# Splitting the large weight pieces with TensorE, and filling the routing lists ten steps earlier

## The chip, the cores and the metric

One core of one Trainium2 chip runs one program. The metric is the device time of one execution in microseconds (us); the time of a kernel is the median of its runs. The kernel before takes 1601.51 us (three runs, 1599.92 to 1602.22).

## The reference

Three layers follow each other on 4608 tokens (8 batches of 576) of width 512. The first is attention over pooled keys: every 8 keys and 8 values are averaged, so each of the 8 heads has 72 of them.

```
k_p = k.reshape(B, H, Sp, 8, D).mean(axis=3);  v_p likewise
attn = softmax(q @ k_p.T / sqrt(D));  x = attn @ v_p          # as rows of 512
```

The second is a feed-forward layer of width 2048 whose activation is a quotient of two polynomials.

```
h = x @ w_in                                   # 512 -> 2048
g = (a0 + a1 h + a2 h^2 + a3 h^3) / (1 + |b0||h| + |b1|h^2 + 1e-6)
x = g @ w_out                                  # 2048 -> 512
```

The third sends each token to one of 8 experts (the largest of 8 logits), runs relu(x @ w1[e]) @ w2[e] with inner width 1024, and scales by the gate.

`w_in` and `w_out` come in 64-bit floats (read as pairs of 32-bit words), all other inputs in 32-bit floats.

## The kernel before, in words

Accuracy is kept by splitting each matrix operand into a high part (float32r, a reduced form that TensorE takes in one pass) and a low part (what the high part leaves over); a product is then three matmuls, high by high, high by low, low by high.

The program has a front, a main loop and a tail. **The front** (before the first `mm1`) does the attention of the first units and turns 24 of the 40 weight pieces into split weights. **The main loop** has steps t = 0, 1, 2, ...; each does one 128-wide slice of the feed-forward layer for a block of 384 tokens (`mm1`, the polynomials in `act_a` to `act_d`, then `mm2` of the slice three steps back, LAG = 3), 16 slices to a block, 12 blocks; attention of later blocks goes on beside it. At the end of a block `evac` copies three results out of PSUM (`y0`, `y1`, `y2`) into buffers of the tag `ys` and writes them to the rows `yd` in DRAM; routing then scatters token numbers into the list `ids`. **The tail** runs the experts.

All engines take their instructions in the order in which the code issues them; nothing is reordered. `point(p)` issues the attention events due at point p (8 points to a unit of 384 tokens and two heads, two points to a step), `tick(c)` issues what is due of the weight pieces at tick c. In the front a tick comes every PACE = 1.3 points from point P0 on, HEAD = 27 ticks in all; from then on there is one tick per step.

A large piece c (c < 24, `j < RING`) is 128 x 512 doubles in a ring of 8 SBUF slots (`sr`). Its chain is spread over the ticks by the table `CONV`:

- tick c: `conv_magnitude` (ScalarE) writes the upper words, scaled, to a PSUM buffer `mag` (tags `y0` to `y3` in turn);
- tick c+1: `conv_sign` (GpSimd) leaves a signed zero in the upper word;
- tick c+2: `conv_join` (VectorE, two instructions) puts sign, exponent and mantissa together as a 32-bit float, into the ring slot for even c and into `mag` for odd c;
- tick c+3: `conv_high` (ScalarE) writes the high part into `wt`; `conv_low` subtracts it from the float and writes the low part, on GpSimd for even c, on VectorE for odd c.

Small pieces (c from 24 on, 128 x 256, buffers `s64` of the tag `ys`) go one tick faster, with the low part on GpSimd. Loads are issued ahead on the DMA queue of SyncE (SP): four ticks ahead for large pieces, one for small ones.

`clear_lists` and `clear_rows` fill `ids` with a mark and the rows of the last two batches in `yd` with zeros: a memset each on GpSimd, then DMAs. They run at step t = NFC + 2 = 18, from two of the three buffers of the tag `ys`, at whose end the first `evac` runs. `kvl` is the pool of three buffers (tag `kv`) into which keys and values are loaded; in the points of steps 8 to 19 no such load is due. `Q`, a PSUM buffer of the tag `y3`, is used by `act_c` in every step of the main loop, and by nothing in the front but `mag`.

Of the kernel before, what the change touches and what calls it, by code (L numbers as in the profile page):

```python
# [9 lines left out]
F32 = mybir.dt.float32  # L10
F32R = mybir.dt.float32r
BF16 = mybir.dt.bfloat16
I32 = mybir.dt.int32
# [3 lines left out]
AF = mybir.ActivationFunctionType  # L17
ALU = mybir.AluOpType
# [91 lines left out]
def tile_kernel(  # L110
# [15 lines left out]
    nc = tc.nc  # L126
    B, H, S, _ = q.shape
    NT, DM = out.shape
    DFF = w_in.shape[1]
    NFC = DFF // 128  # L130
# [14 lines left out]
    one = ctx.enter_context(tc.tile_pool(name="one", bufs=1))  # L145
# [3 lines left out]
    ysp = ctx.enter_context(tc.tile_pool(name="ysp", bufs=3))  # L149
    sm = ctx.enter_context(tc.tile_pool(name="sm", bufs=2))  # L150
    dr = ctx.enter_context(tc.tile_pool(name="dr", bufs=1, space=DRAM))
    py = ctx.enter_context(tc.tile_pool(name="py", bufs=1, space=PSUM))
# [5 lines left out]
    kvl = first.enter_context(tc.tile_pool(name="kvl", bufs=3))  # L158
# [3 lines left out]
    def f32(x):  # L162
        return x.bitcast(F32)
# [8 lines left out]
    def con(name):  # L172
        o, w = cols[name]
        return cst[:, o:o + w]

    ident = con("ident")
    ones = one.tile([G, G], BF16, name="ones")
    nc.vector.memset(ones, 1.0)
    tri = one.tile([G, G], BF16, name="tri")
    make_upper_triangular(nc, tri, val=1.0, diag=False)  # L180
    ab = one.tile([128, 6], F32, name="ab")
# [18 lines left out]

    def clear_lists():
        w = DM
        none = ysp.tile([128, w], I32, tag="ys", name="none")
        nc.gpsimd.memset(none, 2 * NT)
        fill = (E * NT + SL) // 128
        idf = ids.rearrange("(p n) o -> p (n o)", n=fill)
        for o in range(0, 2 * fill, w):
            nc.sync.dma_start(idf[:, o:min(o + w, 2 * fill)], none[:, :min(w, 2 * fill - o)])

    def clear_rows():  # L210
        zero = ysp.tile([96, DM], F32, tag="ys", name="zero")
        nc.gpsimd.memset(zero, 0.0)
        nc.sync.dma_start(yd[(B - 2) * S:, :].rearrange("(p r) c -> p r c", p=96),
                          zero.unsqueeze(1).to_broadcast([96, 2 * S // 96, DM]))
# [13 lines left out]
    wt, cv = {}, {}  # L228
    RING = 6

    def pieces():
        for j in range(NPW):
            w = 512 if j < RING else 256
            for i in range(2):
                for o in range(0, 1024, w):
                    yield j, i, o, w

    PIECES = list(pieces())
# [19 lines left out]
    def words(c):  # L258

        w = cv[c][0].bitcast(U32).rearrange("p (n t) -> p n t", t=2)  # L260
        return w[:, :, 0], w[:, :, 1]

    def conv_magnitude(c):


        j, i, o, w = PIECES[c]
        if i == 0 and o == 0:
            wt[j] = wp.tile([128, 4, 1024], F32R, tag="w", name="wt")
        if j < RING:
            m = py.tile([128, 512], F32, tag=f"y{c % 4}", name="mag")  # L270
        else:
            if "room" not in cv:
                cv["room"] = ysp.tile([128, KD, G], F32, tag="yT", name="mag", bufs=1)
            m = cv["room"][:, c % 2 * 2:c % 2 * 2 + 2].rearrange("p a b -> p (a b)")
        nc.scalar.activation(m, words(c)[1].bitcast(F32), AF.Copy, scale=2.0 ** -112)
        cv[c][1] = m.bitcast(U32)
# [6 lines left out]
    def conv_join(c):  # L283

        (low, up), mag = words(c), cv[c][1]
        nc.vector.scalar_tensor_tensor(out=mag, in0=mag, scalar=3, in1=up,
                                       op0=ALU.logical_shift_left, op1=ALU.bitwise_or)
        out_ = mag if PIECES[c][0] < RING and c % 2 else low
        nc.vector.scalar_tensor_tensor(out=out_, in0=low, scalar=29, in1=mag,
                                       op0=ALU.logical_shift_right, op1=ALU.bitwise_or)  # L290
        cv[c][2] = out_.bitcast(F32)

    def conv_high(c):
        j, i, o, w = PIECES[c]
        nc.scalar.activation(wt[j][:, 2 * i, o:o + w], cv[c][2], AF.Copy)

    def conv_low(c):
        j, i, o, w = PIECES[c]
        (nc.vector if j < RING and c % 2 else nc.gpsimd).tensor_tensor(
            out=wt[j][:, 2 * i + 1, o:o + w], in0=cv.pop(c)[2], in1=f32(wt[j][:, 2 * i, o:o + w]), op=ALU.subtract)  # L300

    CONV = ((0, 0, conv_magnitude), (3, 2, conv_high), (1, 0, conv_sign), (2, 1, conv_join), (3, 2, conv_low))
    TICKS = NCV + 2
    BIG, AHEAD = RING * 4, 4
    loaded = [0]
# [6 lines left out]
    def tick(c):  # L314
        for big, small_, fn in CONV:
            for x in sorted({c - big, c - small_}):
                if 0 <= x < NCV and x == c - (big if x < BIG else small_):
                    fn(x)
        load_to(min(c + AHEAD, max(BIG + 2, c + 1)))
# [215 lines left out]
    def point(p):  # L535
        for fn, U in agenda.get(p, ()):
            fn() if U is None else fn(U)
        if extra and extra[0][0] <= p and (p % 8 in (6, 7) or p > last_unit):
            extra.pop(0)[1](p)
# [4 lines left out]
    def mm1(n, fc):  # L544
        hps = ph.tile([128, N], F32, tag="h", name="hps")
        t, fl = wt[fc // 2], fc % 2
        i, last = 0, 3 * KD - 1
        for wi, xi in ((0, 0), (0, 1), (1, 0)):
            for kk in range(KD):
                nc.tensor.matmul(hps, lhsT=w_in_part(t, wi, kk, fl), rhs=xT[n, kk][:, xi, :],  # L550
                                 start=(i == 0), stop=(i == last))
                i += 1
        return hps

    def act_a(t, hps):
        A = elp.tile([128, N], F32, tag="A", name="A")
        nc.scalar.activation(A, hps, AF.Abs)  # L557
        el[t] = A, hps
# [17 lines left out]
    def act_c(t, part):  # L576

        if part == 0:
            A, C = el[t]
            Q = py.tile([128, N], F32, tag="y3", name="Q")  # L580
            nc.scalar.activation(Q, A, AF.Ln, bias=qone)
            nc.scalar.activation(Q, Q, AF.Exp, scale=-1.0)  # L582
            nc.vector.scalar_tensor_tensor(out=C, in0=C, scalar=a0, in1=Q, op0=ALU.add, op1=ALU.mult)  # L583
            nc.vector.scalar_tensor_tensor(out=Q, in0=A, scalar=qone, in1=Q, op0=ALU.add, op1=ALU.mult)
            el[t] = Q, C
        else:
            Q, C = el[t]
            nc.vector.scalar_tensor_tensor(out=C, in0=Q, scalar=-2.0, in1=C, op0=ALU.add, op1=ALU.mult)  # L588

    def act_d(t):  # L590
        _, C = el.pop(t)
        hi = t3p.tile([128, N], F32R, tag="hi", name="hi")
        lo = t3p.tile([128, N], F32R, tag="lo", name="lo")
        nc.scalar.activation(hi, C, AF.Copy)  # L594
        nc.gpsimd.tensor_tensor(out=lo, in0=C, in1=f32(hi), op=ALU.subtract)  # L595
        gT[t] = hi, lo
# [432 lines left out]


    total = NFC * NBLK
    P0, PACE, HEAD = 4, 1.3, BIG + 3
    c = 0
    for p in range(min(agenda), LEAD):
        if p == min(agenda) + 1:
# [8 lines left out]
    for t in range(total + main.end):  # L1044
        g = t - total - 1
        if g == -NFC:
            first.close()
            p2["one"] = ctx.enter_context(tc.tile_pool(name="p2", bufs=1))
            p2["stg"] = ctx.enter_context(tc.tile_pool(name="stg", bufs=4))
            p2["xr"] = ctx.enter_context(tc.tile_pool(name="xrp", bufs=2))  # L1050
        if t == NFC + 2:
            clear_lists()
            clear_rows()
        point(2 * t + LEAD)
        if t < total:
            hps = mm1(*divmod(t, NFC))
        if g > 0:
            main.high(g)
            main.low(g)
        main.front(g)  # L1060
        if 2 <= t < total + 2:
            act_d(t - 2)
        if 1 <= t < total + 1:
            act_c(t - 1, 0)
        if t < total:
            act_a(t, hps)
        point(2 * t + 1 + LEAD)
        if t < total:
            act_b(t, 0)
        if 1 <= t < total + 1:  # L1070
            act_c(t - 1, 1)
        if t < total:
            act_b(t, 1)
        if g <= 0:
            main.high(g)
        if c < TICKS:
            tick(c)
            c += 1
        if g <= 0:
            main.low(g)  # L1080
        main.prepare(g)
        if LAG <= t < total + LAG:
            mm2(t - LAG)
            n, fc = divmod(t - LAG, NFC)
            if fc == NFC - 1:
                evac(n)
                extra += after_block(n, 2 * t + LEAD + (4 if n < NBLK - 1 else 2))
        main.back(g)
    left = nc.values_load(p2["over"][0:1, 0:1], min_val=0, max_val=NR)  # L1089
# [36 lines left out]
```

## Time and profile before

| | |
|---|---|
| median of 3 runs | 1601.51 us |
| profiled execution | 1602.74 us, of which the span of the trace is 1601.0 us |
| PE busy | 1501.1 us (94% of the span) |
| VectorE (DVE) busy | 1181.1 us (74%) |
| ScalarE (ACT) busy | 1066.4 us (67%) |
| GpSimd (POOL) busy | 756.0 us (47%) |
| mean granted TensorE clock | 0.973 of full speed |

The table is a mean over stages. The 40 slices of the page show the exceptions to a PE that is busy 90% or more: the first four slices (160 us), one slice near 200 us, and the end. PE = TensorE matmuls, PEld = its weight loads, SPq = the DMA queue of SyncE. A granted clock of 1.00 is 2.4 GHz, 0.50 is 1.2 GHz. Line numbers (L299) are those of the kernel before; in rows of the changed kernel's order the same lines stand up to 13 further down.

### The profile page before, as it was taken

The page shows a single profiled execution, that of the slowest core. Times are in us where ns is not written, and L with a number is a line of the kernel's source. Part 1 is how long each engine was busy: PE and PEld are TensorE (multiplying, and loading weights), DVE is VectorE, ACT ScalarE, POOL GpSimd, SP SyncE. Part 2 cuts the span into 40 slices and gives each one's busy share as a digit, 9 for nine tenths or more (in the row PEclk, how much of TensorE's full clock was granted, in tenths as well). Part 3 has the DMA queues.
Part 4 walks back from the last instruction along what each step waited for, and adds up shares of the span by engine and source line. Part 5 has one row for each costly group of instructions (what it writes and reads, how often), then busy time and mean ns, then how long its engine had stood idle before and what let it go on. Part 6 is the DMA issues. An engine that isn't in the chain of part 4 may idle for free. (4 is left out here: it accounts for less than half of the span.)

```text
span 1601.0 us, 25780 instructions
## 1 busy us (share of the span) xinstructions
PE 1501.1 (94%) x8636; PEld 1340.5 (84%) x8636; DVE 1181.1 (74%) x2325; ACT 1066.4 (67%) x2116; POOL 756.0 (47%) x865
## 2 busy tenths in 40 slices
PE   5678979999999999999999999999999999999995
PEld 4567868888889888898888898989899998999994
DVE  5869858878788878878888878778766666666661
ACT  4558856777777777777676777778465556565651
POOL 7958635656455655546565644456121212212210
PEclk9779989999999999999999999999999999999998
DMA  9421131211021111101121101023587777777760
GB/s 291 149 79 57 32 109 31 60 40 46 11 45 36 54 32 40 31 11 56 40 56 33 41 11 31 1 86 93 162 245 258 237 229 246 240 243 237 234 214 19
DMA packets 145995, 166.68 MB, mean 104 GB/s; under 512 B 54719, under 2 KB 97855, under 8 KB 145857
## 3 DMA queue, kind: packets, MB, share of 16 engines
q1 hardware_dynamic: 138624, 145.54, 29.8%
q0 software_dynamic: 7232, 19.44, 3.3%
q8 instruction: 70, 1.15, 0.3%
q14 instruction: 69, 0.56, 0.1%
HBM read 143.37 MB, written 22.09 MB: 103 GB/s over the span
## 5 line engine op out<-in xcount | busy, mean ns | idle before, releaser
L550 PE MATMUL hps<-xT,wt 128*128 128x384 f32 x2304 | 454.4, 346 | 0.0
L550 PEld LDWEIGHTS hps<-xT,wt 128*128 128x128 f32 x2304 | 407.9, 192 | 7.5 <-issue 0.3
L606 PE MATMUL y<-wt,hi 128*128 128x512 f32 x1152 | 372.4, 404 | 11.6 <-ACT ys L619 8.8
L573 POOL TENSOR_TENSOR A<-A,Bt 128x384 f32<-128x384 f32 x192 | 195.1, 1016 | 325.1 <-ACT Bt L572 306.6
L907 DVE TENSOR_TENSOR wt<-ws,wt 128x1024 fp32r<-128x1024 f32 x168 | 203.8, 1225 | 70.5 <-ACT wt L902 65.9
L606 PEld LDWEIGHTS y<-wt,hi 128*128 128x128 f32 x1152 | 204.8, 189 | 51.5 <-ACT ys L619 10.4
L595 POOL TENSOR_TENSOR lo<-C,hi 128x384 fp32r<-128x384 f32 x192 | 198.6, 1034 | 74.7 <-ACT hi L594 45.1
L606 PE MATMUL y<-wt,lo 128*128 128x512 f32 x576 | 227.5, 395 | 0.0
L916 PEld LDWEIGHTS h2ps<-x2T,wt 128*128 128x128 f32 x1632 | 213.0, 190 | 11.6 <-DVE lo L929 0.6
L949 PE MATMUL o<-wt,hi 128*128 128x512 f32 x608 | 220.0, 403 | 0.5 <-ACT hi L928 0.5
L916 PE MATMUL h2ps<-x2T,wt 128*128 128x256 f32 x1632 | 217.5, 283 | 0.5 <-DVE x2T L880 0.3
L583 DVE SCALAR_TENSOR_TENSOR C<-C,ab,Q 128x384 f32<-128x384 f32 x192 | 117.7, 613 | 134.3 <-ACT Q L582 131.3
L594 ACT ACTIVATE hi<-C 128x384 fp32r<-128x384 f32 x192 | 100.2, 522 | 146.6 <-DVE C L588 127.5
L902 ACT ACTIVATE wt<-ws 128x1024 fp32r<-128x1024 f32 x168 | 175.0, 1057 | 0.9 <-DMA ws<-in_moe_w_dram 0.9
L928 ACT ACTIVATE hi<-h2ps 128x256 fp32r<-128x256 f32 x136 | 52.3, 385 | 170.0 <-PE o L949 166.3
L572 ACT ACTIVATE Bt<-A,ab 128x384 f32<-128x384 f32 x192 | 136.5, 711 | 2.7 <-DVE ti L776 2.7
L949 PEld LDWEIGHTS o<-wt,hi 128*128 128x128 f32 x608 | 114.5, 188 | 20.9 <-ACT hi L928 0.7
L565 ACT ACTIVATE C<-hps,ab 128x384 f32<-128x384 f32 x192 | 129.8, 676 | 1.2
L866 POOL DMA_INDIRECT xr<-yd,at x38 | 46.8, 1232 | 174.9 <-PE xps L877 91.7
L606 PEld LDWEIGHTS y<-wt,lo 128*128 128x128 f32 x576 | 108.5, 188 | 24.5
L566 DVE TENSOR_TENSOR C<-C,hps 128x384 f32<-128x384 f32 x192 | 105.0, 547 | 30.0 <-ACT C L565 27.8
L557 ACT ACTIVATE A<-hps 128x384 f32<-128x384 f32 x192 | 93.8, 488 | 43.1 <-PE hps L550 42.1
(381 smaller groups left out, 2500.5 us busy)
## 6 DMA issues: line engine op xcount, KB each, us to landing
ws<-in_moe_w_dram SPq DMA_DIRECT2D x168, 512.0 KB
kt<-in_k_dram SPq DMA_DIRECT2D x64, 144.0 KB
yd<-ys SPq DMA_DIRECT2D x32, 256.0 KB
sr<-in_moe_w_in_dram SPq DMA_DIRECT2D x12, 512.0 KB
sr<-in_moe_w_out_dram SPq DMA_DIRECT2D x12, 512.0 KB
qt<-in_q_dram SPq DMA_DIRECT2D x64, 96.0 KB
vt<-in_v_dram SPq DMA_DIRECT2D x32, 144.0 KB
vt<-in_v_dram SPq DMA_DIRECT2D x32, 112.0 KB
```

The lines of the kernel that those rows point to most:

```text
L550: nc.tensor.matmul(hps, lhsT=w_in_part(t, wi, kk, fl), rhs=xT[n, kk][:, xi, :], start=(i == 0), stop=(i == last))
L565: nc.scalar.activation(C, hps, AF.Identity, scale=a3, bias=a2)
L566: nc.vector.tensor_tensor(out=C, in0=C, in1=hps, op=ALU.mult)
L572: nc.scalar.activation(Bt, A, AF.Identity, scale=b1, bias=b0)
L573: nc.gpsimd.tensor_tensor(out=A, in0=A, in1=Bt, op=ALU.mult)
L583: nc.vector.scalar_tensor_tensor(out=C, in0=C, scalar=a0, in1=Q, op0=ALU.add, op1=ALU.mult)
L595: nc.gpsimd.tensor_tensor(out=lo, in0=C, in1=f32(hi), op=ALU.subtract)
L606: nc.tensor.matmul(yps[n][r], lhsT=g[gi][:, r * G:(r + 1) * G], rhs=w_out_part(w, wi, fl), start=(fc == 0 and i == 0), stop=(fc == NFC - 1 ...
L902: nc.scalar.activation(s["wt"][j][:, 2 * i, :], s["ld"][c], AF.Copy)
L907: nc.vector.tensor_tensor(out=t[:, 2 * i + 1, :], in0=w, in1=f32(t[:, 2 * i, :]), op=ALU.subtract)
L916: nc.tensor.matmul(hps, lhsT=a_, rhs=b_, start=(i == 0), stop=(i == 3 * KD - 1))
L949: nc.tensor.matmul(s["o"][j], lhsT=hl[gi][:, x * 128:(x + 1) * 128], rhs=w_out_part(wt_, wi, fl), start=(first_ and n_ == 0), stop=(last_ ...
```

## The change

The low part of a large piece is no longer subtracted on GpSimd or VectorE. TensorE adds it up in PSUM, the float times the unit matrix `ident`, then the high part times `minus` (the unit matrix times -1), and ScalarE copies it out one tick later (`conv_left`). The sum stands in a single PSUM buffer, tag `y3`; `mag` keeps `y0` to `y2`. The joined float always goes into the ring slot. The front has 28 ticks in place of 27, at 1.25 points each. The two fills run at step 8 in place of 18, from buffers of the tag `kv`.

```diff
+    minus = one.tile([128, 128], F32R, name="minus")
+    nc.scalar.activation(minus, ident, AF.Copy, scale=-1.0)
...
     def clear_lists():
-        none = ysp.tile([128, w], I32, tag="ys", name="none")
+        none = kvl.tile([128, w], I32, tag="kv", name="none")
...
     def clear_rows():
-        zero = ysp.tile([96, DM], F32, tag="ys", name="zero")
+        zero = kvl.tile([96, DM], F32, tag="kv", name="zero")
...
-            m = py.tile([128, 512], F32, tag=f"y{c % 4}", name="mag")
+            m = py.tile([128, 512], F32, tag=f"y{c % 3}", name="mag")
...
-        out_ = mag if PIECES[c][0] < RING and c % 2 else low
-        nc.vector.scalar_tensor_tensor(out=out_, in0=low, scalar=29, in1=mag,
+        nc.vector.scalar_tensor_tensor(out=low, in0=low, scalar=29, in1=mag,
...
     def conv_low(c):
         j, i, o, w = PIECES[c]
-        (nc.vector if j < RING and c % 2 else nc.gpsimd).tensor_tensor(
-            out=wt[j][:, 2 * i + 1, o:o + w], in0=cv.pop(c)[2], in1=f32(wt[j][:, 2 * i, o:o + w]), op=ALU.subtract)
+        x, hi = cv.pop(c)[2], wt[j][:, 2 * i, o:o + w]
+        if j >= RING:
+            nc.gpsimd.tensor_tensor(out=wt[j][:, 2 * i + 1, o:o + w], in0=x, in1=f32(hi), op=ALU.subtract)
+            return
+        left = py.tile([128, 512], F32, tag="y3", name="left")
+        nc.tensor.matmul(left, lhsT=ident, rhs=x, start=True, stop=False)
+        nc.tensor.matmul(left, lhsT=minus, rhs=hi, start=False, stop=True)
+        cv["left", c] = left
+
+    def conv_left(c):
+        j, i, o, w = PIECES[c]
+        if j < RING:
+            nc.scalar.activation(wt[j][:, 2 * i + 1, o:o + w], cv.pop(("left", c)), AF.Copy)
-    CONV = ((0, 0, conv_magnitude), (3, 2, conv_high), (1, 0, conv_sign), (2, 1, conv_join), (3, 2, conv_low))
+    CONV = ((4, 3, conv_left), (0, 0, conv_magnitude), (3, 2, conv_high), (1, 0, conv_sign), (2, 1, conv_join), (3, 2, conv_low))
...
-    P0, PACE, HEAD = 4, 1.3, BIG + 3
+    P0, PACE, HEAD = 4, 1.25, BIG + 4
...
-        if t == NFC + 2:
+        if t == NFC // 2:
             clear_lists()
             clear_rows()
```

TensorE in the front, around the second unit, before. `vps` and `kps` pool values and keys, `qps` and `pps` are transposes, `sps` are scores, `ops` the output of attention.

```order
L411 MATMUL vps<-vt,cst 128x64 x8
L438 MATMUL qps<-cst,qt 128x128 x3
L479 MATMUL pps<-cst,pt 128x128 x3
L479 MATMUL pps<-cst,pt 16x128 x3
L405 MATMUL kps<-cst,kt 64x72 x8
L449 MATMUL sps<-kbd,qT 128x144 x3
```

The same stretch of TensorE's order in the changed kernel:

```order
L424 MATMUL vps<-vt,cst 128x64 x8
L306 MATMUL left<-sr,cst 128x512
L307 MATMUL left<-wt,minus 128x512
L451 MATMUL qps<-cst,qt 128x128 x3
L306 MATMUL left<-sr,cst 128x512
L307 MATMUL left<-wt,minus 128x512
L492 MATMUL pps<-cst,pt 128x128 x3
L306 MATMUL left<-sr,cst 128x512
L307 MATMUL left<-wt,minus 128x512
L492 MATMUL pps<-cst,pt 16x128 x3
L418 MATMUL kps<-cst,kt 64x72 x8
```

Between any two groups of attention matmuls there now stands a pair that needs the piece's float (VectorE), its high part (ScalarE) and the single buffer `left`.

ScalarE in the same stretch of the changed kernel (before, only the `mag` and `wt<-sr` or `wt<-mag` rows stood between those of attention):

```order
L313 ACTIVATE wt<-left 128x512
L277 ACTIVATE mag<-sr 128x512
L296 ACTIVATE wt<-sr 128x512
L453 ACTIVATE qT<-qps 128x384
L313 ACTIVATE wt<-left 128x512
L277 ACTIVATE mag<-sr 128x512
L296 ACTIVATE wt<-sr 128x512
L496 ACTIVATE pT_491<-pps 128x384
L313 ACTIVATE wt<-left 128x512
```

Each tick has one ScalarE instruction more, the copy `wt<-left`, and it stands first in the tick, ahead of `mag` and the high part.

The DMA queue of SyncE from step 6 to step 18, before: `s_...` are loads of small pieces, `qt` of queries, `ys` the rows of the first block.

```order
L255 DMA s_1411<-in_moe_w_out_dram 128x256
L379 DMA qt<-in_q_dram 128x3x64 x2
L255 DMA s_1478<-in_moe_w_out_dram 128x256
L255 DMA s_1548<-in_moe_w_out_dram 128x256
L255 DMA s_1609<-in_moe_w_out_dram 128x256
L379 DMA qt<-in_q_dram 128x3x64 x4
L208 DMA ids<-none 128x512
L208 DMA ids<-none 128x68
L213 DMA yd<-zero 1152x1x512
L622 DMA yd<-ys 128x512 x3
```

The same queue in the changed kernel:

```order
L257 DMA s_1437<-in_moe_w_out_dram 128x256
L210 DMA ids<-none 128x512
L210 DMA ids<-none 128x68
L215 DMA yd<-zero 1152x1x512
L257 DMA s_1500<-in_moe_w_out_dram 128x256
L392 DMA qt<-in_q_dram 128x3x64 x2
L257 DMA s_1567<-in_moe_w_out_dram 128x256
L257 DMA s_1637<-in_moe_w_out_dram 128x256
L392 DMA qt<-in_q_dram 128x3x64 x4
L635 DMA yd<-ys 128x512 x3
```

The three fills moved from just ahead of the first block's rows to a place ahead of the loads of the last three small pieces.

## Rows read from the trace of the kernel before

**Rows 1.** Busy time by engine in stretches; columns as named in the second line.

```profile
core 0: us, PE busy (x) PEld busy (x) DVE busy (x) ACT busy (x) POOL busy (x), PEclk, DMA share, GB/s
12.20:77.70 65.50, 39.08 (x210) 33.64 (x210) 52.82 (x90) 35.23 (x71) 60.79 (x55) 0.85 0.70 223
...
200.00:220.00 20.00, 10.92 (x40) 9.05 (x40) 7.20 (x15) 7.13 (x15) 4.98 (x5) 0.74 0.60 184
```

**Rows 2.** Groups by line, 0 to 180 us; count, then busy us, mean ns, idle before.

```profile
L281 POOL TENSOR_SCALAR sr<-sr 128x512 f32<-128x512 f32 x24 | 37.0, 1566 | 7.8 <-ACT mag L275 7.5
L299 POOL TENSOR_TENSOR wt<-sr,wt 128x512 fp32r<-128x512 f32 x12 | 15.7, 1305 | 2.6 <-DVE mag L289 1.8 <-ACT wt L295 0.5 <-DMA qt<-in_q_dram 0.3
...
L299 DVE TENSOR_TENSOR wt<-mag,wt 128x512 fp32r<-128x512 f32 x12 | 8.2, 684 | 0.1
...
L295 ACT ACTIVATE wt<-mag 128x512 fp32r<-128x512 f32 x12 | 7.1, 592 | 10.7 <-DVE mag L289 10.6
```

**Rows 3.** Timeline, first and last instruction on large pieces; start, us taken.

```profile
8.80 0.62 ACT L275 ACTIVATE mag<-sr 128x512 f32<-128x512 f32 x1 [3.23 <-DMA sr<-in_moe_w_in_dram]
...
77.10 0.68 DVE L299 TENSOR_TENSOR wt<-mag,wt 128x512 fp32r<-128x512 f32 x1
```

**Rows 4.** Timeline of PE, float32 matmuls (two records each) in the front and later.

```profile
28.99 2.18 PE L405 MATMUL kps<-cst,kt 72*64 72x72 f32 x16
31.16 1.81 PE L449 MATMUL sps<-kbd,qT 128*128 128x144 f32 x6
...
193.35 0.90 PE L449 MATMUL sps<-kbd,qT 128*128 128x144 f32 x6
```

**Rows 5.** Timeline of ACT, two instructions that follow without a wait.

```profile
33.22 0.62 ACT L275 ACTIVATE mag<-sr 128x512 f32<-128x512 f32 x1
33.77 0.58 ACT L295 ACTIVATE wt<-mag 128x512 fp32r<-128x512 f32 x1
```

**Rows 6.** Busy time in short stretches, columns as Rows 1 (last row: PE alone).

```profile
50.90:54.30 3.40, 3.40 (x16) 2.96 (x16) 3.33 (x6) 1.63 (x4) 3.08 (x5) 1.00 0.64 220
...
108.90:112.30 3.40, 1.96 (x15) 1.79 (x13) 3.33 (x8) 1.65 (x4) 2.16 (x3) 1.00 0.19 43
569.60:573.10 3.50, 1.74 (x11) 1.44 (x11) 3.50 (x7) 3.43 (x9) 1.59 (x3) 1.00 0.00 0
...
67.90:71.40 3.50, 3.23 (x15) 0.50 0.00 1
```

**Rows 7.** Timeline around the first eviction, of SP, ACT and PE.

```profile
198.91 0.68 SPq L213 DMA_DIRECT2D yd<-zero  x1
...
198.52 0.49 ACT L557 ACTIVATE A<-hps 128x384 f32<-128x384 f32 x1
211.44 0.60 ACT L619 ACTIVATE ys<-y 128x512 f32<-128x512 f32 x1 [10.41 <-DMA yd<-zero]
213.80 0.49 ACT L557 ACTIVATE A<-hps 128x384 f32<-128x384 f32 x1
219.26 0.49 ACT L557 ACTIVATE A<-hps 128x384 f32<-128x384 f32 x1
...
212.09 1.22 PE L606 MATMUL y<-wt,hi 128*128 128x512 f32 x2 [8.78 <-ACT ys L619]
213.11 0.63 PE L606 MATMUL y<-wt,lo 128*128 128x512 f32 x1
```

**Rows 8.** Timeline: a queued key load and its user; a small piece's turn in step 9.

```profile
6.68 0.44 SPq L351 DMA_DIRECT2D kt<-in_k_dram  x1
...
15.19 2.18 PE L405 MATMUL kps<-cst,kt 72*64 72x72 f32 x16 [3.05 <-DMA kt<-in_k_dram]
...
146.99 0.49 ACT L557 ACTIVATE A<-hps 128x384 f32<-128x384 f32 x1
154.37 0.44 ACT L275 ACTIVATE mag<-s 128x256 f32<-128x256 f32 x1
```

**Rows 9.** Timeline: a low part on POOL and the PE group that takes it.

```profile
192.65 1.01 POOL L595 TENSOR_TENSOR lo<-C,hi 128x384 fp32r<-128x384 f32 x1
...
196.89 0.40 PE L606 MATMUL y<-wt,hi 128*128 128x512 f32 x1
```

More of the change, by code (lines that the diff above doesn't have):

```diff
@@ L287, in conv_join @@
                                        op0=ALU.logical_shift_left, op1=ALU.bitwise_or)
-        out_ = mag if PIECES[c][0] < RING and c % 2 else low
-        nc.vector.scalar_tensor_tensor(out=out_, in0=low, scalar=29, in1=mag,
+        nc.vector.scalar_tensor_tensor(out=low, in0=low, scalar=29, in1=mag,
                                        op0=ALU.logical_shift_right, op1=ALU.bitwise_or)
-        cv[c][2] = out_.bitcast(F32)
+        cv[c][2] = low.bitcast(F32)
     def conv_high(c):
```

## The prediction

> **What bounds the kernel now.** I read the busy time by stretches first, to find where PE, the bound of the whole program, is not busy. Two places concern this change. In the front, from the end of the first key pooling to the last low part, 12.2 to 77.7 us, PE works 39.08 us of 65.5 while POOL works 60.79 [rows 1]: POOL sets the pace there, and of its work 37.0 us are sign passes and 15.7 us are the low parts that the change takes away [rows 2]. And near 200 us there is a hole: PE is busy 10.92 of 20 us [rows 1].
>
> Next I read the timelines of both places. Conversion of the large pieces lasts from 8.80 to 77.10 + 0.68 = 77.8 us [rows 3], 2.9 us a piece. In the hole, the absolute value that opens each step's polynomials (L557) starts at 198.52, 213.80 and 219.26: one step takes 15.28 us where the next takes 5.46. ScalarE sat 10.41 us before it could write the third result of the first block, waiting for the DMA of zeros, which holds one of the three `ys` buffers; PE then waited 8.78 us for that copy [rows 7].
>
> Last I read the granted clock. In the front PE ran at half speed almost throughout: three score matmuls take 1.81 us there and 0.90 us later [rows 4], although the column says 1.00 until a first record of the clock exists. It rose near 54 us after a stretch filled wholly with score, output and pooling matmuls, and was back at 0.50 at 67.9 us, where PE was busy 3.23 of 3.5 us and stayed at half speed [rows 6].
>
> **The fills.** With the zeros in a `kv` buffer the eviction finds its three `ys` buffers free. What goes is 15.28 - 5.46 = 9.8 us [rows 7]. That already contains the half-speed matmuls behind the hole (0.63 us for one that otherwise takes 0.40 [rows 7, 9]). Late next at that place is the copy itself, ordinary work of every block, so I subtract nothing more.
>
> At step 8 the same fills cost something else. The zeros take from 198.91 to 211.44, or 12.9 us after that step's L557 [rows 7]. The next entry of the queue is the load of a small piece. The queue hands data over in order: keys issued at 6.68 behind five large loads let PE go on only at 15.19 [rows 8]. So the piece is there about 12.9 us after the L557 of step 8, and ScalarE asks for it 154.37 - 146.99 = 7.4 us after that [rows 8]: it stands still up to 5.5 us, 6.9 with the transfer of the piece (0.26 MB, 1.4 us at the 184 GB/s of the hole [rows 1]). Behind it in ScalarE's order wait the polynomials of the next step, and for those PE. But PE takes each low part 196.89 - 193.66 = 3.2 us after it is ready [rows 9], so at least so much of the delay is covered, and about as much again because the step's own `mm1` input is read before the piece. Loss between 0 and 6.9; I take 1.6, since two covers of about 3.2 leave little but seldom fit exactly. The memsets on POOL (two, of half a microsecond) and the `kv` buffers cost nothing: no load of keys falls into steps 8 to 19.
>
> **The low parts on PE.** Removed: 12 x 1.305 = 15.7 us on POOL and 12 x 0.684 = 8.2 us on DVE [rows 2]. Added: 24 pairs of matmuls and 24 copies on ScalarE. The copy reads PSUM and writes 512 columns to SBUF like the high part of an odd piece, 0.592 us [rows 2]. The first matmul of a pair is a float32 one of 512 columns, which the trace does not show. Bounds: 512/144 of the score matmul, 1.81/3 = 0.60, makes 2.1 us; 512/72 of the key pooling, 2.18/8 = 0.27, makes 1.9 us [rows 4]; I take 1.9, because part of both is fixed, and half of it, 0.95, at full clock. The second is a float32r matmul like those of `mm2`: 0.40 us at full clock, 0.63 at half [rows 7, 9].
>
> The Trainium skill ("FP8 and Floating Point Precision", TensorE Precision Notes) says that true float32 goes through the array in four passes. By that and 1.2 GHz the matmul would take 4 x 512 / 1.2 = 1.71 us, an estimate, and the total below would be some 4 us lower; the two records per float32 matmul and the 0.60 us for 144 columns agree with it.
>
> What matters is less these sums than their order. `left` is one buffer. So a round is: copy, then the float32 matmul, then the matmul of the high part, then the next copy. At half clock: 0.6 + 1.9 + 0.6 + 0.1 for two handovers = 3.2 us. At full clock PE would be done sooner, but the high part is the third instruction of the tick on ScalarE, behind the copy and `mag`; such instructions follow each other at 0.55 us [rows 5]. Then the round is 2 x 0.56 + 0.65 + 0.40 + 0.1 = 2.3 us. The first copy can start at about 15 us (first high part at 13.4, plus the pair). With 23 further rounds the last copy ends at 15 + 23 x 3.2 = 88.6 us at half clock, at 15 + 23 x 2.3 = 67.9 at full clock, if attention did not need PE at all.
>
> It does: 39.1 us at half clock [rows 1], half of that, 19.5, at full clock by the score matmuls [rows 4]. In a round PE is idle 0.7 us (half clock) or 0.95 us (full clock), 16 or 22 us in all. Attention fills these gaps only in part: its groups come in lumps, as value and key pooling back to back, and ScalarE's own attention work stands ahead of the next copy, as the order shows. I take half: 88.6 + 39.1 - 8 = 119.7 us at half clock, 67.9 + 19.5 - 9.8 = 77.6 at full clock. Filled wholly they would be 111.6 and 67.9. Against 77.8 before, this stage becomes 42 us longer (34 at the least) or stays as it is (at best 10 us shorter).
>
> So the relief of POOL is real but is not what the front then waits for. Which clock? In the front only stretches that PE filled without a gap raised it, and rows of both kinds exist for work that fills it in part: busy 1.96 of 3.4 us it kept full speed at 109 us, busy 1.74 of 3.5 it fell at 573 [rows 6]. The new rounds fill PE 2.5 us of 3.2 at half clock, more with attention between, so it should rise; at full clock 1.3 of 2.3 us, so it may fall again. I take half of the front at each: (42 + 0) / 2 = 21 us.
>
> The 28th tick adds one small piece's instructions to the end of the front, by halves of the rows for large ones 1.4 us on POOL at most [rows 2], and takes them from step 14 of the loop, where PE covers them; 0.5 us. The slower spacing of ticks (1.25 points) only keeps the last tick at the same point. `minus` is made while ScalarE waits for its first piece, 3.23 us [rows 3]; nothing.
>
> **The sum.** -9.8 + 1.6 + 21 + 0.5 = +13.3 us. On the profiled execution, 1602.74 us (span 1601.0 and 1.7 around it), that is 1616.0; this execution was 1.2 us over the median of 1601.51, so I predict 1615 us.
>
> **Rivals.**
> - *PE at full clock through the whole front.* Then the stage stays as it is and the fills' gain is kept: -9.8 + 1.6 + 0 + 0.5 = -7.7, 1594 us, faster than before. It needs the clock to rise within the first rounds, by about 25 us, and not to fall until 78. For it: dense 512-column matmuls come every round, as in the stretch before 54 us. Against it: at 67.9 us nearly gapless work did not raise it [rows 6]. The Trainium skill ("TensorE: Matmul & The Clock Gate", What's actually happening) says that sustained matmul activity releases the throttle; read plainly, that rule is this rival, and the last of [rows 6] only half agrees.
> - *PE at half clock throughout.* +42 in the front: -9.8 + 1.6 + 42 + 0.5 = +34, 1636 us. For it: nearly the whole front before ran so. Against it: the new work is denser.
> - *The small piece behind the zeros is not covered.* Then ScalarE's 6.9 us come through in full at step 9 in place of 1.6, on top of the forecast: 1620 us. DVE is busy beside PE in that stage and could not catch up.
>
> **Chances.** Forecast (mixed clock) 0.44, its own range 1604 to 1627; full clock 0.26, 1586 to 1601; half clock throughout 0.20, 1627 to 1645; uncovered piece 0.10. A difference under 0.2% (3.2 us) is about what a measurement of this kernel cannot tell from none. Faster by more: 0.22 of the full-clock case and 0.02 of the mixed one, 0.24. Within: 0.04 of the full-clock case and 0.05 of the mixed one, 0.09. Slower: the rest, 0.67. The range that leaves about a tenth out on each side is 1592 to 1638.
>
> **What would show it.** Right: the step at the first eviction takes 5 to 6 us; the last copy of a low part ends near 98 us, and the first `mm1` starts some 20 us later than before; PE, not POOL, is the busiest engine of the front, and copies wait for PE; the float32 matmul takes 1.7 to 2.1 us a pair of records at half clock. Wrong: rounds of 2.3 us from the beginning (the clock), copies that wait for VectorE or for loads instead (then the single buffer is not the limit), or a new hole of 5 us near step 9.

## The result, and the profile after

The changed kernel takes 1619.1 us (median of four runs, 1614.21 to 1626.56); the kernel before took 1601.66 us beside it. The ratio is 1.0115, 95% interval 1.0073 to 1.0156: slower by 17.4 us. The profiled execution took 1621.09 us, with a span of 1619.0, so the two traces differ by 18.0 us of span.

A convenient ruler is the start of each step's first absolute value on ScalarE (L557 before, L570 now, 192 of them, numbered from 0). Subtracting the old starts from the new ones shows where time comes and goes:

| from | to | before, us | after, us | change |
|---|---|---|---|---|
| start | step 0 | 101.86 | 126.56 | +24.7 |
| step 0 | step 9 | 49.77 | 49.89 | +0.1 |
| step 9 | step 10 | 4.98 | 10.14 | +5.2 |
| step 10 | step 18 | 41.91 | 40.03 | -1.9 |
| step 18 | step 19 | 15.28 | 5.12 | -10.2 |
| step 19 | step 191 | 903.66 | 904.11 | +0.5 |

So the change gains at one place and loses at two. First the front, by busy time in a stretch from 12.2 us to the end of the last copy (columns as in [rows 1]), and the groups by line from 0 to 180 us (the mean ns of one and the idle time before them at the end of a row):

```profile
12.20:99.00 86.80, 70.26 (x282) 38.55 (x282) 43.89 (x78) 47.69 (x92) 46.48 (x43) 0.90 0.54 167
```

```profile
L283 POOL TENSOR_SCALAR sr<-sr 128x512 f32<-128x512 f32 x24 | 37.1, 1559 | 31.6 <-ACT mag L277 31.4
L306 PE MATMUL left<-sr,cst 128*128 128x512 f32 x48 | 35.9, 836 | 15.8 <-ACT wt L313 15.3 <-DVE sr L290 0.5
...
L313 ACT ACTIVATE wt<-left 128x512 fp32r<-128x512 f32 x24 | 14.3, 594 | 24.7 <-PE left L307 24.7
```

In [rows 1] POOL worked 60.79 of 65.5 us and PE 39.08. Now PE works 70.26 of 86.8 and POOL 46.48; the sign passes cost as much as in [rows 2] but stand idle 31.6 us in front of them, and ScalarE's copies wait 24.7 us for PE. PE is now the busiest engine of the stage, and the stage ends at 98.41 + 0.59 = 99.0 us where it ended at 77.8 [rows 3].

The timelines of ScalarE and PE show the round (start, us taken, and in brackets the idle time before and who ended it), at half clock near 20 us and at full clock near 43:

```profile
18.31 0.60 ACT L313 ACTIVATE wt<-left 128x512 fp32r<-128x512 f32 x1 [1.49 <-PE left L307]
18.96 2.07 PE L306 MATMUL left<-sr,cst 128*128 128x512 f32 x2 [0.69 <-ACT wt L313]
20.07 1.39 PE L307 MATMUL left<-wt,minus 128*128 128x512 f32 x1
21.49 0.60 ACT L313 ACTIVATE wt<-left 128x512 fp32r<-128x512 f32 x1 [1.48 <-PE left L307]
...
41.53 0.67 ACT L296 ACTIVATE wt<-sr 128x512 fp32r<-128x512 f32 x1
42.26 0.50 PE L307 MATMUL left<-wt,minus 128*128 128x512 f32 x1
42.79 0.60 ACT L313 ACTIVATE wt<-left 128x512 fp32r<-128x512 f32 x1 [0.59 <-PE left L307]
45.07 0.60 ACT L313 ACTIVATE wt<-left 128x512 fp32r<-128x512 f32 x1 [0.58 <-PE left L307]
```

Copy to copy is 3.18 us at half clock and 2.28 at full. At half clock float32 matmul, high matmul and copy follow each other through the one bank. At full clock the copy waits for a matmul that itself waited for ScalarE's high part of the same tick.

Next the end of the front. The 28th tick brings one more small piece; its load is issued once GpSimd's low part has freed a buffer, and ScalarE waits for it before it goes on with attention:

```profile
97.14 0.92 POOL L303 TENSOR_TENSOR wt<-s,wt 128x256 fp32r<-128x256 f32 x1
98.08 0.35 SPq L253 DMA_DIRECT2D s<-in_moe_w_in_dram  x1
98.41 0.59 ACT L313 ACTIVATE wt<-left 128x512 fp32r<-128x512 f32 x1
100.84 0.43 ACT L277 ACTIVATE mag<-s 128x256 f32<-128x256 f32 x1 [1.85 <-DMA s<-in_moe_w_in_dram]
```

Then the fills at step 8 and, last, the place of the old hole:

```profile
171.37 0.68 SPq L215 DMA_DIRECT2D yd<-zero  x1
175.79 0.35 SPq L257 DMA_DIRECT2D s<-in_moe_w_out_dram  x1
176.45 0.49 ACT L570 ACTIVATE A<-hps 128x384 f32<-128x384 f32 x1
184.51 0.44 ACT L277 ACTIVATE mag<-s 128x256 f32<-128x256 f32 x1 [5.44 <-DMA s<-in_moe_w_out_dram]
186.59 0.49 ACT L570 ACTIVATE A<-hps 128x384 f32<-128x384 f32 x1
...
226.62 0.49 ACT L570 ACTIVATE A<-hps 128x384 f32<-128x384 f32 x1 [0.32 <-PE hps L563]
231.74 0.49 ACT L570 ACTIVATE A<-hps 128x384 f32<-128x384 f32 x1
```

The small piece issued behind the zeros keeps ScalarE idle for 5.44 us, and the step is 5.2 us longer. The step at the first eviction takes 5.12 us instead of the 15.28 of [rows 7].

### The profile page after: what moved, and what is told of

It is laid out like the page before. It is cut to its first block, busy times and chain, and to the rows that moved or that the text cites. A ratio compares the mean times of both kernels' runs of the same rounds, so it can differ in the third digit from the quotient of the medians.

```text
span 1619.0 us, 25964 instructions
## 1 busy us (share of the span) xinstructions
PE 1529.9 (95%) x8708; PEld 1342.4 (83%) x8708; DVE 1173.4 (72%) x2313; ACT 1080.4 (67%) x2141; POOL 743.8 (46%) x853
## 5 line engine op out<-in xcount | busy, mean ns | idle before, releaser
L570 ACT ACTIVATE A<-hps 128x384 f32<-128x384 f32 x192 | 93.8, 488 | 44.9 <-PE hps L563 44.1
```

## The experiments

Theory at the start: the fills are a gain with a collision; the low parts on PE lengthen the front by rounds through a single bank, at a clock that changes on the way. Rivals: the collision is elsewhere, the float32 matmul is the price, ScalarE's order is the round, or all of it is the clock. Step offsets below are against the trace of before. Line numbers differ by a few from kernel to kernel (the copy is L313, L316, L317 or L319); the names of the tiles do not.

**Parts alone.** Before with the fills as in the change:

```
-    none = ysp.tile(..., tag="ys")       +    none = kvl.tile(..., tag="kv")     (zero likewise)
-    if t == NFC + 2:                     +    if t == NFC // 2:
```

> The kernel before with the fills alone changed (step 8, buffers of the keys). Main theory: the step at the first eviction falls from 15.3 to about 5.1 us, and the load of the next small piece waits behind the zeros, so one step near step 9 grows by about 4.8 us: 1601.7 - 10.1 + 4.8 = 1596.4 us. Rival (the transfer is hidden at step 8): 1591.6. Rival (the eviction waits for something else once the buffers are free): 1601 or more.

Measured: 1595.7 us, ratio 0.9968 (0.9957 to 0.998). Steps 18 to 19 give 10.5 us, steps 9 to 10 take 5.4:

```profile
151.20 0.49 ACT L557 ACTIVATE A<-hps 128x384 f32<-128x384 f32 x1
159.50 0.43 ACT L275 ACTIVATE mag<-s 128x256 f32<-128x256 f32 x1 [5.68 <-DMA s<-in_moe_w_out_dram]
161.55 0.48 ACT L557 ACTIVATE A<-hps 128x384 f32<-128x384 f32 x1
```

So the collision belongs to the fills, not to the new front, and ScalarE's wait goes into the step almost whole (5.68 and 5.4). The same with `t == NFC - 2` (step 14):

> The kernel before with the fills from buffers of the keys, but at step 14, behind the load of the last small piece. Main theory: no load is left to wait behind the zeros, and the transfer of 12.5 us is over two steps ahead of the first eviction at step 18: 1601.7 - 10.1 = 1591.6 us. Rival (the zeros also slow loads of queries or cost PE by contention): 1594 to 1597.

Measured: 1587.65 us, ratio 0.992 (0.9906 to 0.9933), faster than both kernels. Steps 9 to 10 are as before, the gain of 10.5 us stays. The median is 4 us better than expected. In the trace about 2 of them appear in the first three steps, with the program still the same there, and 3.9 between steps 19 and 100 (1.0 is lost again by step 191). The next two kernels, which have the old fills, are 3.7 us shorter than before between steps 19 and 100 too, so this part is not the fills'. What it is was not settled.

The change without the new fills (those of before put back):

> The changed kernel with the fills as before (step 18, buffers of the results): the low parts on TensorE alone, with their tick and spacing. Main theory (one buffer, one round after the other): first mm1 about 25 us later than before, 1601.7 + 24.8 = 1626 us, rounds of 3.2 us at half clock and 2.3 at full. Rival (the loss comes from the fills or from the interplay of both): under 1615.

Measured: 1625.04 us, ratio 1.0146 (1.0131 to 1.0162), as the theory said (1626); step 0 starts 29.4 us later and the offset stays between 24 and 30 to the end. And the change's front with the low parts back on GpSimd and VectorE, three banks for `mag`, the 28th tick at 1.25 points:

```
-    left = py.tile(...); nc.tensor.matmul(left, ident, x); nc.tensor.matmul(left, minus, hi)
+    (nc.vector if c % 2 else nc.gpsimd).tensor_tensor(out=wt[j][:, 2*i+1, o:o+w], in0=x, in1=f32(hi), op=ALU.subtract)
```

> As the last one, but the low parts are subtracted on GpSimd (even pieces) and VectorE (odd) as before; three buffers for mag, the float always in the ring slot, 28 ticks at 1.25 points remain, fills as before. Main theory: these side edits cost little, 1602 to 1605 us, first mm1 within 3 us of before. Rival (the tighter buffers of mag or the strided float make the front longer): 1610 or more.

Measured: 1605.99 us, ratio 1.0027 (1.0017 to 1.0037), over the theory's 1602 to 1605 and under the rival's 1610. Conversion ends 1.6 us later than before, but step 0 starts 6.8 us later, not 3. The load of the extra small piece and its user:

```profile
78.93 1.04 POOL L303 TENSOR_TENSOR wt<-s,wt 128x256 fp32r<-128x256 f32 x1
80.00 0.35 SPq L253 DMA_DIRECT2D s<-in_moe_w_in_dram  x1
82.76 0.43 ACT L277 ACTIVATE mag<-s 128x256 f32<-128x256 f32 x1 [5.10 <-DMA s<-in_moe_w_in_dram]
```

Step 15 gives 1.8 us of it back, where the loop now has one piece less. By medians, the low parts alone are 1625.04 - 1605.99 = 19 us, the side edits 5, the fills -5; together 19, measured 17.4.

**The collision in the changed kernel.** After with `t == NFC - 2`:

> After, with the first fills in step 14 instead of step 8 and nothing else changed. Theory (the fills in step 8 delay the load of the small piece that step 9 needs, worth 4.7 to 5.2 us; in step 14 no such load is behind them): step 9 to 10 is back at 5.3 us instead of 10.14, the eviction's step stays at about 5.1 us, and the time is 1619.1 less 5: 1613 to 1615. By the difference of the two runs with before's front (1595.7 and 1587.65) it would be 1611. Rival (the loss at step 9 is only put off, the load waits later): 1618 to 1620.

Measured: 1619.31 us (1614.24 to 1623.55), ratio 1.0116 (1.0095 to 1.0138): no gain in the median, which lies in the rival's range. Yet in its trace the steps 9 to 10 take 5.14 us, and its span is 4.7 us under after's (1614.3 and 1619.0).

```profile
178.11 0.48 ACT L570 ACTIVATE A<-hps 128x384 f32<-128x384 f32 x1
...
183.25 0.49 ACT L570 ACTIVATE A<-hps 128x384 f32<-128x384 f32 x1
```

The collision is gone as the theory has it, and no later step takes the loss over. That the median does not show it fits a front that varies: step 0 is 1.8 us later here than in after, and both kernels' runs spread over 9 to 12 us. This is read from one trace of each kernel; for the medians it is not shown. With before's front the same move is worth 1595.7 - 1587.65 = 8 us.

**What makes the round.** After with the float32 matmul replaced by a second pass of the high part against zeros (the low parts are thereby left out):

```
-    nc.tensor.matmul(left, lhsT=ident, rhs=x, start=True, stop=False)
+    nc.tensor.matmul(left, lhsT=minus, rhs=hi, start=True, stop=False)      # minus = 0 * ident
```

> After, with the float32 matmul of the piece in the low part replaced by a second pass of the high part against a matrix of zeros; the low parts of the large pieces are thereby left out (zeros are written). All waits, banks, copies and the order stay; the first fills stand in step 14. Theory (the two-record float32 matmul of 2.07 us at half and 1.17 us at full clock is what makes the round long): a round loses about 1.6 us at half and 0.7 us at full clock and comes to about 1.6 us, under the 2.2 us that the other engines need of a tick; the last copy ends near 72 to 80 us, and the time is 1587 to 1595. Rival (the hand-over between ScalarE and PE, not the matmul, is the round): the last copy stays beyond 92 us, and the time is over 1606.

Measured: 1624.96 us, ratio 1.0156 (1.0138 to 1.0174); last copy 109.86 + 0.59. The theory fell: with less work on PE the front became longer. The edit is not clean: the cheap matmul reads the high part, so it cannot start before ScalarE has made it, and a plain round is still 3.02 us. And PE's clock stayed at its lower level until after 100 us:

```profile
15.41 0.60 ACT L313 ACTIVATE wt<-left 128x512 fp32r<-128x512 f32 x1 [1.31 <-PE left L307]
18.43 0.60 ACT L313 ACTIVATE wt<-left 128x512 fp32r<-128x512 f32 x1 [1.31 <-PE left L307]
...
100.62 0.80 PE L306 MATMUL left<-wt,minus 128*128 128x512 f32 x1 [1.99 <-ACT wt L296]
...
105.74 0.50 PE L306 MATMUL left<-wt,minus 128*128 128x512 f32 x1 [0.96 <-ACT wt L296]
```

The same instruction takes 0.80 us at 100.62 and 0.50 at 105.74. So float32's own price was not measured. That the clock made this front longer is argued, not shown: a plain round at half clock is even a little shorter than in after (3.02 and 3.19 us), but 22 of the 24 pairs ran at half clock. Whether it stayed there for the lighter work or for the matrix of zeros was not separated.

After with two banks for `left` (`tag=f"y{2 + c % 2}"`, the magnitudes on two banks and a spare tile), fills in step 14:

> After, with two banks for `left` in turn instead of one (the magnitudes give one of their three banks up and take the room buffer every third time), and the first fills in step 14. Theory (chain through one bank): float32 matmul of the next piece need no longer wait for the copy of the last one, so a round falls from 3.19 us to the longer of PE's share (2.07 + about 0.4 for the high matmul, 2.5 us) and ScalarE's at half clock, and the last copy ends near 83 to 88 us instead of 99.0; the time is 1597 to 1604. Rival (ScalarE's own chain of magnitude, eviction and copy in the order of the tick sets the round, the bank is incidental): rounds stay near 3.2 and 2.3 us, the last copy near 99, and the time is 1611 to 1615.

Measured: 1608.99 us, ratio 1.0043 (1.0027 to 1.006), between the theory's range and the rival's. The rounds say why:

```profile
16.07 0.60 ACT L317 ACTIVATE wt<-left 128x512 fp32r<-128x512 f32 x1 [0.88 <-PE left L311]
18.67 0.60 ACT L317 ACTIVATE wt<-left 128x512 fp32r<-128x512 f32 x1 [0.88 <-PE left L311]
...
26.16 0.60 ACT L317 ACTIVATE wt<-left 128x512 fp32r<-128x512 f32 x1 [0.59 <-PE left L311]
28.44 0.60 ACT L317 ACTIVATE wt<-left 128x512 fp32r<-128x512 f32 x1 [0.60 <-PE left L311]
```

At half clock a round falls from 3.19 to 2.60 us: there the bank was the chain. At full clock it stays at 2.28: there it is ScalarE's own order, high part, PE, copy. These are plain rounds, those without attention in them. The last copy is at 96.76 + 0.59, where 83 to 88 were expected. In the one-bank kernel with the same fills it is at 100.01 + 0.59, and there the pair still took 2.07 us at 49.00, here 1.17 from 22.41 on, with some at half clock later; so what two banks give the whole front is not shown.

To undo ScalarE's order as well, the copy is moved one tick later, `(5, 4, conv_left)`, with a 29th tick (1.2 points each):

> The kernel with two banks for `left` (e6_two_banks, 1608.99 us), with the copy of a low part one tick later: ScalarE then copies the result of a matmul that had a whole tick to end, and no longer waits inside its own chain (high part, TensorE, copy, magnitude, next high part), which still took 2.60 us a round at half clock and 2.29 at full with two banks. The last copy needs a 29th tick, so one more small piece comes to the front. Theory (that chain through ScalarE sets the plain rounds): plain rounds fall to ScalarE's own 1.9 us or GpSimd's 1.9, the last copy ends at 86 to 92 us (96.8 + 0.6 in e6_two_banks), and the time is 1601 to 1606, the 29th tick's 3.5 to 5 us counted. Rival (the long rounds of 3.8 to 8.0 us, in which the attention's matmuls stand ahead of the low part in TensorE's order, set the front): their sum stays, the last copy ends at 94 to 98 us, and with the 29th tick the time is 1609 to 1613.

Measured: 1602.87 us, ratio 1.0015 (1.0002 to 1.0028), in the theory's range; last copy 87.05 + 0.59. ScalarE's copies no longer wait for PE:

```profile
34.15 0.58 ACT L317 ACTIVATE wt<-left 128x512 fp32r<-128x512 f32 x1
...
35.73 0.60 ACT L317 ACTIVATE wt<-left 128x512 fp32r<-128x512 f32 x1
```

A plain round is 1.58 us, and still the front is 10 us longer than before: thirteen of its 23 rounds take 2.06 to 7.61 us, 54.6 of 70.6 us together, and in those that have a chunk of attention's matmuls the low part stands behind it in PE's order. So the long rounds that the rival named are there as well.

**How much of it is the clock.** After with the fills in step 14 and 16 matmuls of ones ahead of PE's first work, read by nobody (lines shortened):

```
+    warm = ysp.tile([128, 512], F32R, tag="ys"); nc.vector.memset(warm, 1.0)
+    for x in range(16): nc.tensor.matmul(heat, lhsT=warm[:, 0:128], rhs=warm, start=x == 0, stop=x == 15)
```

> After with the first fills in step 14 (e8_after_step14, 1619.31 us), and 16 matmuls of ones (float32r, 512 columns, 0.63 us each at half clock, 10 us) on TensorE before its first work, into the bank of `left`, read by nobody: they fill the time in which TensorE waits for keys. Theory (the long front is a matter of the clock: in e8_after_step14 the float32 pair took 2.07 us until 51 us and 1.17 after, and in e7_cheap_difference, with less work on TensorE, the high matmul stayed at half speed until 102 us and the front was longest): the clock is up from about 13 us, plain rounds take 2.3 us from the first on, the long rounds of 8.0 and 5.7 us become 4.6 to 5.0, the last copy ends at 85 to 91 us instead of 100.6, and the time is 1604 to 1611. Rival (rounds are too thin to hold the clock, and it is back at half by 25 us): 1616 to 1623.

Measured: 1609.49 us, ratio 1.0045 (1.003 to 1.006), against 1619.31 without them: 9.8 us. In the trace the pair takes its full-clock time and the rounds are 2.28 us from the first on:

```profile
15.05 0.60 ACT L319 ACTIVATE wt<-left 128x512 fp32r<-128x512 f32 x1 [0.98 <-PE left L313]
17.33 0.60 ACT L319 ACTIVATE wt<-left 128x512 fp32r<-128x512 f32 x1 [0.58 <-PE left L313]
...
86.62 0.59 ACT L319 ACTIVATE wt<-left 128x512 fp32r<-128x512 f32 x1
...
17.98 1.17 PE L312 MATMUL left<-sr,cst 128*128 128x512 f32 x2 [0.69 <-ACT wt L319]
```

The Trainium skill ("TensorE: Matmul & The Clock Gate", What's actually happening) says that activity of PE releases its throttle; this run agrees, while in the run with the zeros PE worked in every round and was at half clock until after 100 us. The traced execution is the fastest of six. Those at a mean granted clock of 0.981 and 0.984 took 1604.90 and 1603.77 us, the four at 0.976 to 0.978 took 1608.89 to 1610.46: the clock differs between executions of one program, and in these six the time goes with it.

This puts the run with two banks and the later copy in another light. Its clock was up early too, with the pair at 1.06 to 1.17 us from 20.23 us on but for one, and its last copy ends where the one of the run with ones ahead ends, at 87.64 and 87.21 us:

```profile
20.23 1.17 PE L310 MATMUL left<-sr,cst 128*128 128x512 f32 x2
...
87.05 0.59 ACT L317 ACTIVATE wt<-left 128x512 fp32r<-128x512 f32 x1
```

So with the clock up, the second bank and the later copy made the plain rounds shorter and the front hardly: ten plain rounds fell from 22.8 to 16.0 us together, and the other thirteen grew from 48.8 to 54.6. What that run gained over the one-bank kernel (1602.87 and 1619.31 us) cannot be told apart from the clock.

The same 16 matmuls ahead of before's front, with the fills in step 14:

> Before with the first fills in step 14 in the keys' buffers (e2_fills_step14, 1587.65 us), and the same 16 matmuls of ones on TensorE before its first work. Theory (in this front GpSimd sets the pace and TensorE waits for it, so its clock is worth nothing until the last low part at 77 us; only the attention and routing behind it, to the first step at 100.9 us, gain): the last low part stays at 75 to 78 us, the first step is 0 to 4 us earlier, and the time is 1583 to 1588. Rival (the attention's matmuls at half clock hold the conversion too, through ScalarE's and VectorE's waits for them): the last low part ends at 70 to 73 us, and the time is 1576 to 1582. If the clock falls back before 30 us, 1587 to 1589.

Measured: 1591.51 us, ratio 0.9936 (0.9923 to 0.9949), 3.9 us over the same kernel without them, and out of every range given, nearest to the last one. There the column shows the lower level again soon (busy time, PE first, granted clock third from the end):

```profile
12.00:16.00 4.00, 1.86 (x16) 1.72 (x16) 2.56 (x5) 2.07 (x4) 3.76 (x3) 1.00 1.06 336
16.00:20.00 4.00, 2.18 (x16) 1.97 (x16) 3.32 (x6) 2.50 (x5) 4.00 (x4) 0.51 1.01 325
```

Here the clock was back at its lower level by 16 to 20 us, after a stretch in which PE was busy 1.86 of 4 us. The last low part ends at 78.25 + 0.68, 1.1 us later than in before. Since the clock did not stay up, what a full clock would be worth to this front is not shown. Against the trace without the ones, step 0 is 1.4 us later and step 19 is 2.9 us later; where the rest lies was not settled.

**Half of the pieces.** Only the even pieces on PE, copied a tick later; odd ones subtracted on VectorE:

```
+        if c % 2:
+            nc.vector.tensor_tensor(out=wt[j][:, 2*i+1, o:o+w], in0=x, in1=f32(hi), op=ALU.subtract); return
```

> After, with only the even ones of the large pieces (12 of 24) left to TensorE and ScalarE; the odd ones have their low part subtracted on VectorE as in before. The first fills stand in step 14, in the keys' buffers. Theory (the front is a chain through the one bank `left`: copy, float32 matmul, high matmul, copy, 3.19 us at half and 2.28 us at full clock): that chain now has two ticks for each round, some 4.9 us at before's 2.43 us a tick, so it no longer sets the pace; the last low part of a large piece then ends at 74 to 80 us (77.8 in before, 99.0 in after), and the front costs only its 28th tick (3.5 to 5 us). Sum: 1587.65 of before with the fills in step 14, plus 3.5 to 5: 1591 to 1593. Rival (PE's own work, or ScalarE's eviction, is what is short at half clock, not the chain): half the work of it stays, so about half of the +21 us, and the time is 1598 to 1603. If GpSimd's relief counts (it loses its 12 subtractions of 1.3 us), up to 8 us less than the theory's: 1584.

Measured: 1598.29 us, ratio 0.9985 (0.9974 to 0.9997), at the rival's lower end, 10.6 us over before's front with the same fills. The last copy is at 85.05 + 0.58, the last low part on VectorE ends at 86.65, and step 0 starts 12.3 us later. Groups of ScalarE from 12 to 90 us, then PE and VectorE between 42 and 52:

```profile
L277 ACT ACTIVATE mag<-sr 128x512 f32<-128x512 f32 x22 | 13.9, 633 | 19.5 <-DVE sr L290 11.7 <-POOL sr L283 2.4 <-DMA sr<-in_moe_w_in_dram 2.3
L316 ACT ACTIVATE wt<-left 128x512 fp32r<-128x512 f32 x12 | 7.0, 582 | 0.0
```

```profile
42.27 2.08 PE L309 MATMUL left<-sr,cst 128*128 128x512 f32 x2 [4.52 <-ACT wt L316]
...
46.81 3.68 PE L427 MATMUL vps<-vt,cst 128*128 128x64 f32 x16
...
50.60 0.29 DVE L428 TENSOR_TENSOR va<-vps,cst 128x128 f32<-128x128 f32 x1 [6.36 <-PE vps L427]
...
51.53 0.69 DVE L290 SCALAR_TENSOR_TENSOR sr<-sr,mag 128x512 uint32<-128x512 uint32 x1
```

No copy waits for PE, and yet the front is long. PE stands 4.52 us until ScalarE's copy has freed `left` for the next pair; attention's pooling of values (`vps`) comes behind that pair in PE's order; VectorE stands 6.36 us for it, and the joins of the next pieces stand behind attention's value copy in VectorE's order. ScalarE's magnitudes then wait for the joins. The pair shown ran at half clock (2.08 us), so order and clock were not separated in this run.

## Why the prediction was right, point by point

Sign, size and range came out: 1615 us (1592 to 1638) was forecast, 1619.1 measured, inside the forecast's own 1604 to 1627. By its terms, from the profiled executions (+13.3 forecast, +18.4 up to step 191):

- *First eviction, -9.8.* Measured -10.2, and -10.5 in the fills' own runs. Mechanism and size were right.
- *Small piece behind the zeros, +1.6.* Measured +5.2. The load was late by the reckoned amount (idle 5.44 us, reckoned 5.5 without the transfer); wrong was the step "PE takes each low part 196.89 - 193.66 = 3.2 us after it is ready [rows 9], so at least so much of the delay is covered". Next to nothing was covered: 5.44 us of waiting made the step 5.2 longer here, 5.68 made it 5.4 longer with the fills alone. What happened is the rival of the uncovered piece. A wait on an engine that feeds the bound should be counted whole unless a row shows what the bound does meanwhile.
- *Front, +21.* The last copy ended at 99.0 us (98 forecast) and 21.2 us later than before; rounds were 3.19 and 2.28 us (3.2 and 2.3). That PE replaces POOL as the busiest engine and the copies wait for PE is in the groups above. The float32 matmul gives two records, 2.07 us together at half clock, the forecast's upper bound being 2.1; copy, float32 matmul and high matmul together fill the round as reckoned. The other estimate given for it, 1.71 us, was too low, and it would have lowered the total by 2.2 us (half of 23 x 0.19), not by some 4.
- *Inside that term two errors cancelled, which was luck.* At full clock half of attention's work was taken as filling PE's gaps. In the traced run with ones ahead, at full clock for most of the front, 23 rounds took 86.62 - 15.05 = 71.6 us; plain rounds would be 23 x 2.28 = 52.4, so the rounds with attention in them cost 19.1 us more, about all of the 19.5 that the prediction had for it and not half. The full-clock end was thus some 10 us too early (77.6 forecast, 87.2 measured). The rival at full clock, 1594 us, would not have come out even with its condition nearly met: that execution took 1603.77 us, with no collision in step 9. On the other side the clock was up for more than the half that was taken: in after's trace 15 of the 24 pairs take their full-clock time (1.06 to 1.17 us), those from 36 to 75 us and the last two from 93. With the forecast's own 119.7 us for the other 9 this would make 99.4 us, an estimate; no run held this front at half clock throughout.
- *A reading for that rival.* It was to be supported by "dense 512-column matmuls", "as in the stretch before 54 us". That stretch held score, output and pooling matmuls of 72 to 384 columns.
- *28th tick, +0.5.* Wrong by its size: 3.5 us (24.7 - 21.2) lie between the last copy and step 0, of which step 15 gives 1.6 back. The step that failed counted only the extra instructions; the wait is for a load that cannot be issued before GpSimd frees the buffer. With the old low parts it is 5.2 us.

Of the signs named ahead, the step of 5 to 6 us, the last copy near 98, the busiest engine and the pair's time came true. So did one named as wrong: a hole of 5 us near step 9.

What stays open: why executions of the same front raise the clock at different times, what the second bank and the later copy are worth at an equal clock in the medians, and the 4 us by which before's front with the fills in step 14 beat its forecast.

## What to carry to other kernels

Relieving the busiest engine of a stage did not pay here, because the work landed in the queue of an engine whose order ties two streams together: before, conversion did not use PE at all; after the move, conversion and attention waited for each other's turn there. Half of the low parts were enough to end the conversion 9 us later. A second buffer and a step of slack shorten the plain round of a hand-over (at full clock from 2.28 to 1.58 us), but the stage went by its long rounds and in the two traces at full clock it ended at the same time with and without them (87.6 and 87.2 us). So add up the long rounds before mending the plain one, and compare two kernels only after looking at the clock of both. And a big transfer goes where no small, soon-needed load is issued behind it: moving the fills alone, to step 14, made the fastest kernel of all (1587.65 us).

## What the runs showed of the hardware

The clock of the front is no constant. Three kernels with the same front (the change, the change with the old fills, the change with fills in step 14) show the float32 pair at half speed until different times, in one execution each:

```profile
36.06 1.12 PE L306 MATMUL left<-sr,cst 128*128 128x512 f32 x2
```

```profile
41.59 2.07 PE L306 MATMUL left<-sr,cst 128*128 128x512 f32 x2 [0.69 <-ACT wt L313]
45.80 1.17 PE L306 MATMUL left<-sr,cst 128*128 128x512 f32 x2 [1.07 <-ACT wt L313]
```

```profile
49.00 2.07 PE L306 MATMUL left<-sr,cst 128*128 128x512 f32 x2 [0.69 <-ACT wt L313]
...
58.07 1.14 PE L306 MATMUL left<-sr,cst 128*128 128x512 f32 x2 [0.84 <-ACT wt L313]
```

In the first it is at full speed by 36.06 us, in the second between 41.59 and 45.80, in the third between 49.00 and 58.07. The changed kernel's runs spread over 12.4 us (1614.21 to 1626.56), where before's spread over 6 (1598.54 to 1604.58 over all its runs); that the clock makes this spread is likely by the six executions with ones ahead, but not shown for this kernel. The Trainium skill ("TensorE: Matmul & The Clock Gate", What you observe) says that the moment of the change varies from run to run, by 500 ns either way under sustained activity. These rows agree that it varies, but by more than ten microseconds in a front whose work comes in rounds; the measurement decides.
